# An adaLN transformer block on one core: V projected first, fewer filling matmuls, sums of four norms on VectorE, a new order

## The chip, the core and the metric

The kernel runs on one core of a Trainium2 chip. Its engines run side by side, each through its own queue of instructions in order: TensorE (PE in the profile, with PEld for its weight loads), VectorE (DVE), ScalarE (ACT), GpSimd (POOL) and SyncE (SP). ACT and SP also issue the transfers (DMA); these stand in the engine's queue like any other instruction. Matmul results land in PSUM, which DVE and ACT read. The metric is the device time of one execution in microseconds (us); lower is better.

## What is computed

A sequence of 2048 tokens of width 448 goes through a block of attention and feed-forward. A vector c gives six modulation vectors: shift and scale for each norm, and a gate for each half. Attention is local and dilated: each of 16 heads of width 28 looks at 8 tokens, two apart, its own included.

```python
    x = A_x
    mod = (_silu(c) @ w_mod).reshape(c.shape[0], 6, 1, -1)
...
    h = _layernorm(x, axis=-1) * (1 + ca) + sa
    x = x + ga * _A_ref(h, A_wqkv, A_wo)
    h = _layernorm(x, axis=-1) * (1 + cb) + sb
    x = x + gb * _B_ref(h, B_w1, B_w2)
```

`_A_ref` projects to Q, K and V with `wqkv`, takes a softmax over the positions 0, 2, ..., 14 behind each token, and projects with `wo`; `_B_ref` is silu(h `w1`) `w2` with a hidden width of 1792. sa, ca, ga, sb, cb, gb are the six parts of `mod`.

Tensors are bfloat16, sums are kept in float32.

## The kernel before

**Tiling.** Even and odd tokens are two streams of 1024, since the dilation is 2 and the streams never meet. The first part of the work goes in four chunks of 256 token pairs (`NC = 4`): load of x, first norm, Q/K projection. V and the attention go in nine units (`NU = 9`) of two windows of 57 queries and 64 keys. The second half goes in eight blocks `m` of 128 token pairs for the output projection and second norm, and in four groups `k` for the FFN.

**Names of the steps**, with the lines of the profile:

- Loads (L240): `ldx0a`, `ldx0b`, `ldx1` to `ldx3` (x), `ldc` (c), `ldm_a0/1` (the part of w_mod with the first shift and scale, 672 and 224 KB), `ldm_b0/1` (the rest, 1344 and 448 KB), `ldwqk0/1`, `ldwv0/1`, `ldwo0/1`, `ldw1..`, `ldw2..`. Each is one issue on SP or ACT.
- `tab` is ACT's table load, `silu_c` (L299) the silu of c, `ccol` (L303) four tiny matmuls that lay it out, `scT` its copy. `mod1.mm` and `mod2.mm` (L319, 32 matmuls each) give shift and scale in columns, `ga.mm` and `gb.mm` (L337) the gates.
- `warm` and `junk0` to `junk21` (L294) are the filling matmuls: on a zeroed tile, into a PSUM tile that nobody reads.
- First norm of block `m`, `n1m`: `st0/1` (L358, L359: bn_stats and bn_aggr on DVE), `rstd` (L371, L372 on POOL), `nm`, `xn0/1` (L390 on ACT or L392 on DVE: the normalized rows). The first two blocks are turned on TensorE (`h00.trp`, `h01.trp`, L451), and the modulation is applied on the way out of PSUM: `h00.mod0/1`, `h01.mod0/1` (L235 on ACT, L237 on DVE), two quarters of the width each. Later blocks are turned by DMA (`.tr`, L409) and modulated in place.
- `pad0..3` (L437) spread the Q/K weights to heads of 32 columns. `qkKg.S/.C` (L478) project chunk K, head group g, in two halves of 8 and 6 matmuls; `.ev` (L482) takes the result out of PSUM. `vU.S/.C` (L495) project V of unit U in 16 and 12 matmuls; `.ev` (L500).
- `lgU` (L533) logits of unit U, into two PSUM tiles; `exU0/1` (L540) exponentials on ACT, one for each tile; `mkU` (L591) mask; `avU` (L607) product with V; `rcU`, `onU` (L614, L619) division; `otrU` (L622) DMA transpose; `alU` (L628) copy into place.
- `woM.S/.C` (L658) output projection of block M, `resM` (L666) residual on DVE, which leaves the row sums beside it. Second norm `n2m`: either `s`: `mean` (L365) from those sums and two squares on ACT (`sq`, L368), or `b`: bn_stats on DVE as in the first norm. `HOW2` says which for each block.
- `gK.mod` modulation, `f1Ki` (L687) first FFN matmuls of group K, 7 pairs, with silu out of PSUM on ACT (L692); `f2M` (L712, and L724 in the last block) second FFN matmuls; `yaM` (L747) residual; `stoM` (L752, L754) store.
- At the end a check that no softmax sum left its range: `checkmm`, `flag`, and `read`, which every engine executes (L831), ahead of a branch to a slower version.

**Order.** Each step is an object in a list; its number is its place there. The string `ORDER` names all of them in the order in which they are emitted, each with a letter for its engine (p PE, a ACT, v DVE, g POOL, s SP). It fixes every engine's queue; waits between engines follow from the data. There are four PSUM tiles, handed out and taken back in that order, so a matmul step also waits for the engine that empties the tile it gets.

The order before begins so. TensorE: `warm`, three `junk`, `ccol`, ten `junk`, `mod1.mm`, `h00.trp`, `h01.trp`, nine `junk`, the eight halves of `qk0`, `v0`, `v1`, `lg0`, then `qk1` mixed with `lg1`. ACT: `ldx0a`, `ldx0b`, `ldm_a0`, `ldwqk1`, `tab`, `silu_c`, `scT`, `ldwv1`, `n10.xn0/1`, `pad2`, `h00.mod0`, `h01.mod0`. SP: `ldc`, `ldx1`, `ldm_a1`, `ldwqk0`, `ldx2`, `ldwv0`, `ldx3`. DVE takes `h00.mod1` and `h01.mod1`.

Of the kernel before, what the change touches and what calls it, by code (L numbers as in the profile page):

```python
# [39 lines left out]
23g 30p 21g 34p 27g 36p 40p 0a 64v 63v 1a 3a 2s 8a 20a 69v 70v 53a 54p 55a 6a 9s 33p 4s 41p 44p 7s 65g 29g 37p 49p 52p 35p 66v 67a 71g 72g 112v 111v  # L40
73v 74v 39p 42p 68a 38p 57p 75p 78p 58v 10s 5s 62v 47p 51p 32p 61a 50p 48p 24g 43p 46p 76a 77v 80v 45p 31p 11s 59v 60v 105v 106v 79a 113g 15a 85p 114g
115a 86g 168v 93p 116a 118s 87p 107g 94g 169v 108v 109v 110a 210v 163v 162v 117s 81p 89p 82g 95p 22g 90g 25g 26g 83p 88a 91p 12s 164g 13s 96a 97p 101p
98g 102g 92v 56v 84a 250p 251a 252a 165v 119v 122v 121v 99p 103p 100a 120v 127p 123p 166v 104v 28g 170g 171v 167a 172v 211v 173v 259p 124g 128g 129p
125p 260a 261a 131p 132g 135p 253v 126a 130a 205v 204v 174s 175s 136g 133p 262v 134a 137p 138a 143p 254p 206g 139p 140g 144g 177a 178v 212g 179v 255v
256v 263p 145p 141p 147p 146a 16s 14s 149p 264v 265v 176v 213v 214v 142a 148a 273p 150a 180p 184p 207v 181g 182p 185g 274a 275a 183a 287p 208v 209v
288a 289a 215v 186p 153v 154v 192p 188p 193g 217s 216s 266s 257s 194p 276v 220a 221v 187v 219v 189g 290v 190p 277p 196p 195a 267a 258a 278v 279v 218v
191a 200p 197g 198p 201g 202p 291p 199v 203a 268p 292v 293v 301p 269g 270p 302a 303a 19s 280s 281v 230p 272v 282p 271v 231g 343g 283g 315p 284p 304v
316a 232p 286v 285v 350v 226p 233v 305p 227g 317a 228p 345a 344a 306v 294s 295v 318v 352a 229a 351a 17s 18s 222p 223g 234p 235g 224p 307v 346g 236p
347g 225v 308s 237a 319p 348a 320v 353g 354v 321v 246p 247g 329p 248p 238p 239g 330a 249a 331a 242p 240p 156v 309v 349v 243g 322s 357s 355v 356v 241a
151p 244p 332v 333p 310p 152v 323a 155v 358s 324p 311g 334v 335v 336s 362v 312p 314v 313v 161v 444v 296p 325g 326p 297g 359a 361a 360a 245a 298p 299v  # L50
300v 159v 437v 327v 363p 364g 445a 383p 365p 384g 366a 385p 387p 388g 386a 367p 389p 368g 446a 337v 158v 328v 338p 375p 447g 376g 369p 377p 439a 390a
# [90 lines left out]
def layer(ctx, tc, io, safe):  # L142
# [13 lines left out]
    def ct(shape, name, dt=BF16):  # L156
        return const.tile(shape, dt, name=name)
# [15 lines left out]
    junk = ct([128, 512], "junk")  # L173
# [26 lines left out]
    ps = [psum.tile([128, 2, 512], F32, name=f"ps{i}") for i in range(4)]  # L200
# [20 lines left out]
    P = Plan()  # L221
# [66 lines left out]
    misc_ready = [pool_op("rcone", lambda: G.memset(rc[:], 1.0), "rcone"), pool_op("ones", ones, "ones")]  # L288

    def warm_up(o, n):  # L290
        t = ps[w_first["slot"]["ps"][0]]
        for _ in range(n):
            for j in range(2):
                matmul(t[:, j, :], lhsT=junk[half(j), 0:128], rhs=junk[half(j)], start=True, stop=True)  # L294
# [4 lines left out]
    sc_op = P.op("silu_c", "a", "silu_c", lambda o: S.activation(out=sc7[:], in_=c7[:], func=ACTF.Silu), [ld_c, tab])  # L299
# [475 lines left out]
    for k in range(1, NC):  # L775
# [6 lines left out]
        if k == 1:  # L782
# [3 lines left out]
            eng = {"dve": V, "pool": G}  # L786
# [101 lines left out]
```

## Time and profile before

| | us |
|---|---|
| median of 3 runs | 179.65 (178.55 to 180.41) |
| the profiled execution | 179.35 |
| its span, first to last instruction | 177.5 |
| outside the span | 1.85 |
| mean granted clock of TensorE | 0.979 |

The profile is of one execution. Its busy times are for an engine's instructions, and those of PE overlap a little, since matmuls are pipelined. A row of the timeline gives start, length, engine, line, operation, tiles and count; in brackets the idle time of the engine before it and who ended it. Lines that carry the argument are shown in the prediction.

### The profile page before, as it was taken

To read this page: it belongs to the slowest core of one execution; us is meant where nothing else is said; L and a number is where in the kernel's file an instruction comes from. 1 tells how busy PE (TensorE), PEld (TensorE's weight loads), DVE (VectorE), ACT (ScalarE), POOL (GpSimd) and SP (SyncE) were. 2 spreads that over 40 slices of the span, in tenths; PEclk is the share of its full clock that TensorE was granted. 3 is DMA by queue.
4 is the path that set the end of the run, shared out by engine and by line. 5 is a ranking of instruction groups with operands and counts; after the bars stand their busy time and mean duration, and the time that the engine had idled before them with its cause. 6 is when DMAs were issued, how large, how long until landed. Compare 5 with 4: busy or idle time off the path is not lost.

```text
span 177.5 us, 6130 instructions
## 1 busy us (share of the span) xinstructions
PE 161.1 (91%) x2716; PEld 84.3 (47%) x2716; DVE 84.6 (48%) x186; ACT 101.0 (57%) x136; POOL 23.6 (13%) x68
## 2 busy tenths in 40 slices
PE   7885998996899999989999999999999999999920
PEld 2252454453465555635555644455444444554710
DVE  3929579585678887696053870050623000020420
ACT  3345488974785868399896768967144662400000
POOL 7722260110000140001110400013000000000000
PEclk9998799999999999999999999999999999999995
DMA  5993792979965976630009038300140000010240
GB/s 185 392 357 84 145 375 65 140 242 92 153 185 109 289 150 80 134 59 4 0 21 105 4 59 199 34 2 4 42 128 4 0 0 4 0 52 4 103 153 21
DMA packets 32351, 18.54 MB, mean 104 GB/s; under 512 B 25022, under 2 KB 31294, under 8 KB 32318
## 3 DMA queue, kind: packets, MB, share of 16 engines
q1 hardware_dynamic: 30334, 15.67, 38.7%
q10 hardware_dynamic: 1984, 2.41, 4.3%
q8 instruction: 23, 0.38, 0.9%
q14 instruction: 10, 0.08, 0.2%
HBM read 10.21 MB, written 1.84 MB: 68 GB/s over the span
## 4 chain that ended last, share of the span: by engine, by line
PE 77%; DMA 8%; ACT 5%; DVE 3%; issue 3%; ACTq 1%; DVEq 0%
PE ps L687 24%; PE ps L712 21%; PE ps L478 15%; DMA wqk<-in_A_wqkv_dram 5%; PE ps L658 4%; PE ps L495 4%; PE ps L533 3%; PE ps L724 3%; PE ps L607 3%; DMA h<-xn 3%; ACT p L540 1%; ACT h L235 1%; ACT ho L235 1%; PE ps L337 1%; ACTq L240 1%
## 5 line engine op out<-in xcount | busy, mean ns | idle before, releaser
L712 PE MATMUL ps<-w,both 64*128 64x448 bf16 x392 | 39.2, 349 | 0.0
L692 ACT ACTIVATE both<-ps 128x1024 bf16<-128x1024 f32 x28 | 27.6, 1021 | 19.6 <-PE ps L687 19.5
L687 PEld LDWEIGHTS <-w 64*128 64x128 bf16 x392 | 19.8, 94 | 23.1 <-issue 1.8
L478 PE MATMUL ps<-ho,wp 64*128 64x512 bf16 x224 | 27.6, 395 | 3.2 <-ACT ho L235 2.5
L712 PEld LDWEIGHTS <-both 64*128 64x128 bf16 x392 | 19.0, 94 | 17.9
L747 DVE TENSOR_TENSOR ot<-ps,x_all 128x896 bf16<-128x896 f32 x6 | 6.5, 1090 | 38.1 <-issue 20.6
L687 PE MATMUL ps<-h,w 64*128 64x512 bf16 x196 | 23.0, 376 | 0.8 <-issue 0.5
L687 PE MATMUL ps<-wqk,w 64*128 64x512 bf16 x196 | 22.3, 376 | 0.0
L540 ACT ACTIVATE p<-ps 128x912 bf16<-128x912 f32 x18 | 15.9, 929 | 7.8 <-PE ps L533 7.8
L478 PEld LDWEIGHTS <-wp 64*128 64x128 bf16 x224 | 12.0, 98 | 16.5 <-issue 3.5
L482 ACT CAST qk<-ps 128x1024 bf16<-128x1024 f32 x12 | 11.8, 1014 | 5.4 <-PE ps L478 5.4
L495 PE MATMUL ps<-wv,ho 64*64 64x448 bf16 x252 | 13.7, 352 | 0.0
L666 DVE SCALAR_TENSOR_TENSOR x_all<-ps,x_all 128x448 bf16<-128x448 f32 x16 | 9.5, 619 | 8.5 <-PE ps L658 8.5
L591 DVE TENSOR_TENSOR p<-p,maskb 128x1824 bf16<-128x1824 bf16 x9 | 10.1, 1121 | 5.4 <-ACT p L540 5.3
L390 ACT ACTIVATE xn<-x_all,nm,rs 128x512 bf16<-128x512 bf16 x12 | 9.4, 811 | 4.9 <-POOL nm L380 2.7
L658 PE MATMUL ps<-wo,ho 64*128 64x448 bf16 x112 | 12.2, 350 | 0.0
L372 POOL TENSOR_TENSOR rs<-rs,negh 128x2 f32<-128x2 f32 x16 | 11.3, 708 | 1.3
L368 ACT ACTIVATE scr<-x_all,mv 128x448 bf16<-128x448 bf16 x16 | 10.6, 665 | 0.9 <-POOL mv L365 0.7
L371 POOL TENSOR_SCALAR rs<-mv 128x2 f32<-128x2 f32 x16 | 3.1, 197 | 56.6 <-ACT scr L368 21.0
L358 DVE BATCH_NORM_STATS2 st<-x_all 128x6 f32<-128x448 bf16 x16 | 9.7, 605 | 1.9 <-DMA x_all<-in_A_x_dram 1.9
L619 DVE TENSOR_TENSOR o<-ps,rc 121x896 bf16<-121x896 f32 x9 | 9.8, 1091 | 0.3
L294 PE MATMUL ps<-junk 64*128 64x512 bf16 x56 | 8.8, 472 | 1.2 <-DVE junk L202 1.2
(79 smaller groups left out, 144.7 us busy)
## 6 DMA issues: line engine op xcount, KB each, us to landing
w<-in_B_w_dram SPq DMA_DIRECT2D x2, 896.0 KB, 5.4
w<-in_B_w_dram SPq DMA_DIRECT2D x2, 784.0 KB, 7.5
x_all<-in_A_x_dram SPq DMA_DIRECT2D x3, 448.0 KB, 8.3
both<-in_w_mod_dram SPq DMA_DIRECT2D x1, 1344.0 KB, 6.6
out_dram<-ot SPq DMA_DIRECT2D x6, 224.0 KB, 1.9
both<-in_w_mod_dram ACTq DMA_DIRECT2D x1, 672.0 KB, 6.9
x_all<-in_A_x_dram ACTq DMA_DIRECT2D x2, 224.0 KB, 3.2
wqk<-in_A_wqkv_dram ACTq DMA_DIRECT2D x1, 448.0 KB, 8.9
```

What stands on the lines that cost most here:

```text
L368: S.activation(out=scr[:], in_=x_all[:, us[t], :], func=ACTF.Square, bias=mv[:, t, 0:1], accum_out=mv[:, t, 1:2])
L372: G.tensor_tensor(out=rs[:], in0=rs[:], in1=negh[:], op=ALU.pow)
L478: return [matmul(t[:, j, :], lhsT=w, rhs=hT[rows, :, kt, s0:s0 + CP], start=start, stop=stop)]
L482: copy_on(o)(out=qk[:, :, g, :, s0:s0 + CP], in_=t[:].rearrange("p j (t s) -> p j t s", t=2))
L495: return [matmul(t[half(par), j, 0:D], lhsT=hT[rows, par, kt, k0:k0 + KB], rhs=wv[rows, kt, :], start=start, stop=stop) for par in range(2)]
L540: S.activation(out=p_of[u][:, 2 * t * w:2 * t * w + 2 * w].rearrange("p (j n) -> p j n", j=2), in_=bank(a, t)[:, :, 0:w], func=ACTF.Exp, s ...
L591: V.tensor_tensor(out=p, in0=p, in1=m, op=ALU.mult)
L619: V.tensor_tensor(out=dims(t[0:n, :], 0, (576, 2), (DH, H), (1, DH)), in0=view(bank(a))[:, :, :, 0:DH], in1=r, op=ALU.mult)
L658: x = matmul(t[:, par, 0:D], lhsT=oT[rows, par, i // 2, 128 * m:128 * m + 128], rhs=wo[rows, j, :], start=(j == 0), stop=(j == 5))
L687: return [matmul(t[:, i // 7, :], lhsT=w1[rows, kt, 128 * i:128 * i + 128], rhs=h[rows, :, kt, :], start=start, stop=stop)]
L692: S.activation(out=hid[:, k % 2, :, i, :], in_=t[:], func=ACTF.Silu)
L712: x = matmul(t[:, par, 0:D], lhsT=hid[half(hf), k % 2, jj, ii, 128 * j:128 * j + 128], rhs=w2[half(hf), ii + 7 * jj, :], start=(way == 0 a ...
```

## The change

Four things change. `HOW2` puts the sums of the last four second norms (blocks 4 to 7) from ACT's squares to bn_stats on DVE. The `junk` steps may be put on SP, where they do nothing; 17 of the 22 are. `ORDER` is a new one. With `HOW2` the list has four steps fewer, so the numbers behind that place shift.

```diff
-HOW2 = "ssssssss"
+HOW2 = "ssssbbbb"
...
 ORDER = """
...
     def warm_up(o, n):
+        if o["eng"] == "sp":
+            return
         t = ps[w_first["slot"]["ps"][0]]
         for _ in range(n):
             for j in range(2):
                 matmul(t[:, j, :], lhsT=junk[half(j), 0:128], rhs=junk[half(j)], start=True, stop=True)
     w_first = P.op("warm", "p", "warm", lambda o: warm_up(o, WARM), take=("ps",), group=("P", "w", 0))
-    junks = [P.op(f"junk{i}", "p", "junk", lambda o: warm_up(o, 1), [w_first], group=("P", "w", 0)) for i in range(JUNK)]
+    junks = [P.op(f"junk{i}", "ps", "junk", lambda o: warm_up(o, 1), [w_first], group=("P", "w", 0)) for i in range(JUNK)]
```

The new order in names, where it differs most:

```text
PE, start    ccol warm junk16 junk19 junk10 junk6 mod1.mm h00.trp h01.trp junk0 v0.S v1.S v0.C v1.C
             qk00.S qk02.S qk01.S qk03.S qk02.C qk01.C qk03.C qk00.C ga.mm mod2.mm lg0 lg1
             qk11.S qk13.S qk10.S qk11.C qk12.S qk10.C qk13.C qk12.C av1 v2.S lg2 v2.C av0 v3.S gb.mm lg3
ACT, start   ldc tab ldm_a1 silu_c ldm_a0 ldwqk1 ldwqk0 ldm_b1 ldm_b0 n10.xn0 n10.xn1 n11.xn1
             h00.mod1 pad3 pad2 n12.xn0 v1.ev qk02.ev qk01.ev qk00.ev ex00 ex01 ex10 ex11
SP, start    ldx0a ldx0b ldx1 ldwv0 ldwv1 ldx2 n12.tr n13.tr ldx3 ldwo0 n15.tr n14.tr
DVE, start   n10.st0 n10.st1 n11.st1 n11.st0 n10.nm scT n12.st0 n11.nm n11.xn0 n12.st1 mod1.ev
             h00.mod0 h01.mod1 h01.mod0 pad0 pad1 n13.st0 n13.st1 n12.xn1 v0.ev n13.xn0 n13.xn1
POOL, start  rcone vone0 ozero0 masks n10.rstd n11.rstd ozero1 n12.rstd
PE, to FFN   wo1.C qk33.S qk31.S qk33.C qk31.C av3 v6.S av4 v6.C v8.S v7.S v8.C v7.C lg5
             qk30.S qk32.S wo2.S qk32.C qk30.C wo2.C f100.S lg6 f100.C f102.S f105.S wo3.S
PE before    wo1.C qk32.C qk31.S av4 qk31.C qk30.S qk33.S qk30.C qk33.C av5 v8.S lg6 v8.C v6.S v7.S v6.C
             mod2.mm v7.C av6 wo3.S wo4.S wo3.C wo2.S wo4.C wo2.C f100.S
end, SP      sto4 sto6 read sto5 sto71        (before: sto4 sto0 sto6 sto3 read sto72)
end, ACT     sto70 read sto72                 (before: sto71 read sto70)
```

More of the change, by code (lines that the diff above doesn't have):

```diff
@@ new lines @@
+42s 98g 101p 38s 99p 25g 102g 29g 23g 103p 43s 113g 81p 89p 90g 104a 100v 85p 93p 91p 94g 86g 114g 115v 82g 87p 116v 56v 92a 88a 95p 83p 147p 151p 10s
+168v 169v 117s 163v 162v 170g 171g 84a 172v 96v 250p 148v 152v 259p 118s 120v 121v 122v 119v 164g 11s 211v 165v 251a 252a 260a 261a 210v 166v 127p
+135p 123p 15a 128g 124g 136g 129p 131p 167a 130a 125p 137p 173v 205v 204v 262v 132g 253v 133p 14s 263p 175s 126a 134a 212g 139p 174s 140g 138v 273p
+264v 265v 213v 17a 141p 177v 254p 274a 206g 142a 255v 256v 214v 176v 275a 179v 143p 178a 149p 144g 150a 287p 145p 288a 146a 215a 289a 266s 257s 207v
@@ L61 @@
+583v 581v 543p 584v 535p 493s 536a 605p 597p 606g 598g 544a 589p 607p 608a 590g 593p 599p 594g 600a 585p 586g 595p 591p 592a 596a 609p 610g 587p 611p
+549p 558p 550p 551p 612a 588a 613p 552g 601p 559p 602g 603p 553p 560p 561g 554p 562p 614p 604a 563p 615p 564p 616g 617p 618p 619p 555p 622p 623p 624p
+625p 620v 556v 565v 557s 626v 621s 628v 627a 630v 633p 634v 635p 566s 631a 629s
 """
```

35 lines of the change are left out of this document (14 added, 21 removed).

## The prediction

> **What bounds the kernel now.** I read four views in this order: the page's shares and slices, the busy time by stretch, the chain of waits, and the timeline of the first 15 us.
>
> First the page: busy time of each engine, and the transfer rate in 40 slices of 4.44 us.
>
> ```profile
> PE 161.1 (91%) x2716; PEld 84.3 (47%) x2716; DVE 84.6 (48%) x186; ACT 101.0 (57%) x136; POOL 23.6 (13%) x68
> ...
> GB/s 185 392 357 84 145 375 65 140 242 92 153 185 109 289 150 80 134 59 4 0 21 105 4 59 199 34 2 4 42 128 4 0 0 4 0 52 4 103 153 21
> ```
>
> TensorE (PE) is busy 91% of the span, but that hides where it is not. The stretches show it; columns are length, then busy us (instructions) of PE, PEld, DVE, ACT, POOL, then granted clock, DMA share, GB/s.
>
> ```profile
> 0.00:15.06 15.06, 10.75 (x109) 4.93 (x110) 8.44 (x27) 5.70 (x10) 7.67 (x30) 1.00 0.78 275
> 15.06:23.25 8.19, 8.13 (x60) 3.76 (x63) 5.16 (x16) 4.94 (x7) 2.77 (x7) 0.79 0.69 164
> 23.25:78.03 54.78, 50.44 (x1428) 28.51 (x1425) 42.33 (x81) 39.46 (x52) 6.66 (x14) 1.00 0.76 162
> 78.03:164.14 86.11, 86.11 (x1080) 43.05 (x1080) 25.17 (x58) 50.87 (x70) 6.52 (x18) 1.00 0.18 34
> 164.14:169.66 5.52, 5.52 (x46) 4.06 (x44) 2.18 (x2) 0.00 (x0) 0.00 (x0) 1.00 0.26 99
> 169.66:177.50 7.84, 0.11 (x2) 0.00 (x1) 1.27 (x4) 0.00 (x0) 0.00 (x0) 0.74 0.28 87
> ```
>
> From 15.06 (first Q/K projection) to 169.66 (last matmul) PE is the bound: 154.60 us, of which it idles 0.06 + 4.34 + 0 + 0 = 4.40. Before lie 15.06 us of loads, first norm and filling matmuls; behind, a tail of 7.84. So only four things can move the end: the start of useful matmuls, the clock, the 4.40 of idle, the tail.
>
> The clock, in stretches cut where it changes:
>
> ```profile
> 12.97:16.39 3.42, 1.27 (x11) 0.65 (x13) 3.34 (x11) 1.95 (x4) 0.00 (x0) 1.00 0.12 24
> 16.39:19.80 3.41, 3.41 (x19) 1.50 (x17) 3.27 (x12) 1.90 (x3) 0.90 (x2) 0.50 0.73 180
> 40.27:43.69 3.42, 2.14 (x70) 1.27 (x71) 1.87 (x3) 1.60 (x3) 0.00 (x0) 1.00 1.20 119
> ```
>
> After a stretch in which PE was busy 1.27 of 3.42 us the granted clock is 0.50 for 3.41 us, which costs 3.41 x 0.5 = 1.7 us of the first Q/K projection. After one with 2.14 busy of 3.42 it stayed at 1.00.
>
> The chain of waits and the timeline say what sets 15.06:
>
> ```profile
> 11.93 1.02 ACT ho L235 x2
> ...
> 12.98 1.38 DVE ho L237 x4
> ```
> ```profile
> 1.24 4.02 PE L294 MATMUL ps<-junk 64*128 64x512 bf16 x18 [1.24 <-DVE junk L202]
> ...
> 1.69 0.46 ACTq L240 DMA_DIRECT2D both<-in_w_mod_dram  x1
> ...
> 3.62 0.38 SPq L240 DMA_DIRECT2D x_all<-in_A_x_dram  x1
> ...
> 4.01 0.26 ACT L299 ACTIVATE sc<-c 7x64 bf16<-7x64 bf16 x1
> ...
> 6.74 1.52 ACT L390 ACTIVATE xn<-x_all,nm,rs 128x512 bf16<-128x512 bf16 x2 [1.07 <-DVE nm L378]
> ...
> 8.68 0.95 PE L319 MATMUL ps<-scT,both 128*128 128x1 bf16 x32 [0.60 <-DMA both<-in_w_mod_dram]
> ...
> 9.49 1.05 PE L451 MATMUL ps<-ident,xn 128*128 128x128 bf16 x16
> ...
> 10.48 2.12 PE L294 MATMUL ps<-junk 64*128 64x512 bf16 x18
> ...
> 11.09 0.94 ACT L437 COPY wp<-wqk 128x896 bf16<-128x896 bf16 x1 [2.83 <-DMA wqk<-in_A_wqkv_dram]
> ...
> 14.44 0.56 ACT L235 ACTIVATE ho<-ps,modc 128x256 bf16<-128x256 bf16 x1 [1.50 <-DVE ho L237]
> ...
> 15.06 8.15 PE L478 MATMUL ps<-ho,wp 64*128 64x512 bf16 x56 [2.46 <-ACT ho L235]
> ```
>
> w_mod lands at about 8.6, the modulation columns (L319) and transposes (L451) follow by 10.54; ACT first pads the late Q/K weights (L437), and only then the modulated rows are written, ACT and DVE taking turns (L235, L237, with waits of 1.50), until 15.06.
>
> **The change, part by part.**
>
> *V first.* Its 56 matmuls (two window pairs) need wv and the four modulated parts, not the Q/K weights. These rows price it:
>
> ```profile
> 23.13 1.71 PE L495 MATMUL ps<-wv,ho 64*64 64x448 bf16 x32
> ...
> 25.40 1.33 PE L495 MATMUL ps<-wv,ho 64*64 64x448 bf16 x24
> ```
> ```profile
> x_all<-in_A_x_dram SPq DMA_DIRECT2D x3, 448.0 KB, 8.3
> ...
> both<-in_w_mod_dram ACTq DMA_DIRECT2D x1, 672.0 KB, 6.9
> ...
> wv<-in_A_wqkv_dram ACTq DMA_DIRECT2D x1, 224.0 KB, 7.0
> ```
> ```profile
> SPq L240 <- DMA x_all<-in_A_x_dram: 1.9, 2, 1.0
> ```
>
> Start: on ACT the 672 KB of w_mod now stand behind the silu of c, so they are issued after c has landed, near 3.6 instead of 1.69 (the 3.62 row also shows the ninth transfer waiting for an early one; this may be the ninth). By the slices 0.82 MB move by 4.44 and 0.39 MB a us after that. Ahead of w_mod's end lie x0 0.448, x1 0.448, wv 0.448 and w_mod 0.896, 2.24 MB: 4.44 + 1.42/0.39 = 8.1; with x2 too, 9.2. I take 8.5, next to today's 1.69 + 6.9 = 8.6. Then 0.95 (L319) to 9.45 and half of the 1.05 (L451) to 10.0. DVE writes two parts of the first 128 tokens in 0.69 (half of 1.38), then ACT two in 1.02, since the rows show the two engines taking turns on one PSUM tile; the second tile's parts fall to DVE alone, beside ACT. V starts at 10.0 + 0.69 + 1.02 + 0.2 for hand-overs = 11.9. Lower end 11.2 (no turn-taking, w_mod at 8.1); upper end 13.4 (all four strictly in turn). I take 11.9 because the second tile belongs to one engine.
>
> Queues that these steps move past: SP now carries x0, x1, wv and x2 ahead of the first transposes, and x3 behind them, where it is needed first at about 25. POOL sets rc before the first norm's root instead of at 25:
>
> ```profile
> 25.02 0.52 POOL L288 MEMSET rc<- 128x288 f32 x1 [1.39 <-PE ps L495]
> ```
>
> That puts ACT's two normalized rows at 7.2 instead of 6.74, to 8.7, still 0.7 ahead of the transposes at 9.45.
>
> V lasts 1.71 + 1.33 = 3.04, to 14.9, and Q/K follow without a gap: the Q/K weights (0.896 MB) land at 4.44 + (2.24 + 0.448 + 0.896 - 0.82)/0.39 = 11.5, their pads end by 11.75 + 2 x 0.94 = 13.6 on ACT. The cover is 1.3 us. So useful work starts 15.06 - 11.9 = 3.16 us earlier. V is moved, not added; where it stood (23 to 27, under the table load and exponentials) TensorE then has a gate and the second modulation columns, which it does today at 38 to 40 and 70 to 71: no more in sum. Their 1.79 MB of w_mod land at about 4.44 + (3.58 + 1.79 - 0.82)/0.39 = 16.1 and are needed at 21.4.
>
> *Filling matmuls.* 17 of 22 become nothing: 34 of 56 matmuls. The 20 that stand between c's columns and L319 take 20 x 4.02/18 = 4.5 us at the slow pace, from about 3.8 to 8.3, so they hide in the wait for w_mod. One pair stands before V; PE then waits about 10.8 to 11.9. In any 3.41 us PE idles at most some 1.3, nearer the 2.14-busy row than the 1.27-busy one, so I take clock 1.00 and the 1.7 us come back. Ends: 0 back, 1.7 back.
>
> The Trainium skill's "TensorE: Matmul & The Clock Gate" (section "What's actually happening") says that the clock falls only after an idle window of about 3.4 us. The trace disagrees: it fell after a wait of 2.46. By that page a wait of 1.1 is safe, as by my rows, and the sum stays. The same section asks for a busy window of about 3.4 us before the clock rises; by that rule 4.5 us of filling hold a whole window only if its phase is kind, and otherwise V starts slowly, the rival below with 176.6.
>
> *Sums on DVE for the last four second norms.* It removes 8 squares on ACT and adds 8 statistics on DVE:
>
> ```profile
> L368 ACT ACTIVATE scr<-x_all,mv 128x448 bf16<-128x448 bf16 x16 | 10.6, 665 | 0.9 <-POOL mv L365 0.7
> ...
> L358 DVE BATCH_NORM_STATS2 st<-x_all 128x6 f32<-128x448 bf16 x16 | 9.7, 605 | 1.9 <-DMA x_all<-in_A_x_dram 1.9
> ...
> L359 DVE BATCH_NORM_AGGREGATE mv<-st 128x2 f32<-128x6 f32 x16 | 2.9, 182 | 0.5
> ```
>
> 8 x 0.67 = 5.3 us leave ACT (50.87 busy of 86.11 there) and 8 x 0.79 = 6.3 come to DVE (25.17 of 86.11). PE idles 0.00 in that stretch: worth 0, covered by DVE's 61 us of slack. Without the cover the FFN's next block would wait, up to 6.3.
>
> *New order up to the first FFN.* From 15.06 to 78.03 it is one in-order puzzle of four PSUM tiles. Now both first logits run back to back and hold all four tiles, so the next four Q/K halves wait for exponentials; in return the first FFN matmul comes before one more logits, two attention products and two output projections, PE work that then fills later waits:
>
> ```profile
> L658 PE MATMUL ps<-wo,ho 64*128 64x448 bf16 x112 | 12.2, 350 | 0.0
> ...
> L533 PE MATMUL ps<-qk 28*64 28x57 bf16 x576 | 6.9, 200 | 2.9 <-issue 2.9
> ...
> L607 PE MATMUL ps<-v,p 64*57 64x29 bf16 x576 | 6.0, 179 | 0.0
> ```
>
> Two of 8 projections, one of 9 logits, two of 9 products: 3.05 + 0.77 + 1.33 = 5.2 us. I cannot show the new idle from a row. Low end 1, if every wait is filled; high end 9, if the stretch doubles its 4.34. I take 4.4, what the same work idles today.
>
> *Tail.* Today the last stores are:
>
> ```profile
> 170.70 1.35 ACTq L754 DMA_DIRECT2D out_dram<-wqk  x2
> ...
> 171.96 0.34 SPq L754 DMA_DIRECT2D out_dram<-wqk  x1
> ```
>
> SP issues its last one at 171.96, behind the read of the flag. In the new order a 224 KB store stands between that read and SP's last: one more issue, 0.4 us (0 to 0.8).
>
> *Sum.* V at 11.9, plus PE work 154.60 - 4.40 - 1.70 = 148.5, plus idle 4.4, gives 164.8; plus tail 7.84 + 0.4 = 173.0. The profiled execution took 179.35 for a span of 177.5, 1.85 outside: 174.9. That execution is 0.3 under the median 179.65.
>
> **The rivals.**
>
> *The clock falls or never rises ahead of V.* For: far fewer filling matmuls. Against: the 40.27 row. V's start falls into a slow window: + 1.7, 176.6; two windows, 178.3.
>
> *The new order idles more.* PE's gain only meets ACT or DVE: for it, DVE is busy 42.33 and ACT 39.46 of 54.78 in that stretch, and four tiles are all there is. Idle 8.4 instead of 4.4: 178.9, no change. Both would have to fit into the 47 us from 21.4 to 68. Against: with 5.2 us of PE work and what hangs on it moved behind, each stays near four fifths.
>
> *The new order idles less.* Idle 1 to 2: 171.5 to 172.5. For: nothing after 78.03 waits today, and of the 4.34 ahead of it 1.28 lie in one place, the 40.27 row.
>
> *Slower: the first norm is held on ACT's queue.* Its first two normalized rows (6.74, 1.52) now stand behind seven transfer issues on ACT. If a transfer from the ninth on waits for the one eight before it (3.62 row), the last issue could wait for Q/K weights at 11.5: rows to 13.7, transposes to 14.2, modulation to 16.2, V at 16.4, and PE waits of 4 and 2 us, thus the slow clock: 174.9 + 4.5 + 1.7 = 181.1. It decides against the change once V starts after about 14.9 with a slow window, or 16.4 without. Against: counting in order, that last issue waits for an early x or V transfer, landed by about 8.
>
> *By the page "DMA: Bandwidth & Descriptors" (section "Queues, rings and completion order") of the Trainium skill* each engine serves the two queues in turn, so fetching V's weights and x first would slow w_mod; the 8.1 to 9.2 above holds that already.
>
> **How the numbers follow.** A measurement of this kernel tells about 1% from no change (177.9 to 181.4). Chances: forecast 0.50 (own range 173 to 177), clock 0.12, more idle 0.18, less idle 0.10, ACT's queue 0.10. Faster by over 1%: 0.50 + 0.10 + 0.08 of the clock case = 0.68. Within: 0.04 of clock and 0.15 of more idle = 0.19. Slower: 0.03 + 0.10 = 0.13. The range 171.0 to 179.5 takes in less idle, clock and most of more idle, and leaves out ACT's queue and the extremes.
>
> **What would show each step.** V's matmuls (L495) first at 11.2 to 13.4, Q/K (L478) right behind within 0.3; L319 at 8.1 to 9.2; granted clock 1.00 from V on; the first FFN matmul (L687) near 11.9 + (8.13 + 50.44 - 1.7 - 5.2) + 4.4 = 68 instead of 78.03; PE without a wait from there on; no ACT squares among the last four norms; 8.2 from last matmul to end. I am wrong if Q/K wait for their weights, if the clock reads 0.50 after 11.9, or if idle after V's start exceeds 8.

## The result and the profile after

The changed kernel took 185.38 us (median of 4 runs, 184.57 to 188.53), the kernel before 179.53 on the same chip: ratio 1.0315, 95% interval 1.0259 to 1.0371. Here and below a median takes all runs of a kernel, and a ratio only the runs within 1.5% of the kernel's fastest, so the two can differ by up to 1%. The forecast was 174.9, and its range ended at 179.5. So the change is 3% slower, and the forecast missed by 10.5 us. The profiled execution took 184.65 for a span of 182.9.

The page of the changed kernel, the same lines as before: shares, granted clock in 40 slices (4.57 us each), transfer rate.

```profile
PE 160.1 (87%) x2682; PEld 83.3 (46%) x2682; DVE 90.9 (50%) x208; ACT 97.0 (53%) x120; POOL 21.4 (12%) x62
...
PEclk9965999996999789999999999999999999999995
...
GB/s 183 309 401 314 117 189 109 99 232 61 127 103 388 150 0 103 134 4 0 4 84 79 77 64 56 4 77 138 52 162 4 4 0 0 4 0 4 100 68 50
```

PE's share fell from 91 to 87% although its work did not grow. The clock line has dips in three places instead of one. The stretches (length, then busy us of PE, PEld, DVE, ACT, POOL, granted clock, DMA share, GB/s) tell where:

```profile
0.00:14.37 14.37, 7.81 (x75) 4.09 (x75) 7.36 (x24) 4.22 (x6) 8.47 (x29) 0.88 0.88 302
14.37:25.01 10.64, 10.64 (x115) 4.87 (x114) 9.22 (x24) 5.74 (x8) 3.38 (x11) 0.84 0.70 214
25.01:40.00 14.99, 12.15 (x421) 7.82 (x420) 11.38 (x26) 11.55 (x14) 1.88 (x4) 1.00 0.66 146
40.00:50.15 10.15, 7.96 (x236) 4.45 (x237) 5.37 (x10) 5.80 (x9) 0.00 (x0) 0.83 0.62 92
50.15:61.67 11.52, 8.80 (x82) 4.04 (x82) 5.78 (x10) 6.17 (x7) 0.00 (x0) 1.00 0.96 257
61.67:78.55 16.88, 16.37 (x414) 8.97 (x415) 12.96 (x29) 12.01 (x19) 1.77 (x4) 0.90 0.40 65
78.55:174.76 96.21, 96.21 (x1347) 49.10 (x1342) 37.59 (x86) 51.48 (x62) 5.92 (x14) 1.00 0.21 44
174.76:182.90 8.14, 0.11 (x2) 0.00 (x1) 1.27 (x4) 0.00 (x0) 0.00 (x0) 0.71 0.23 66
```

From 78.55 on, PE waits for nothing, as forecast. Ahead of it lie idle times of 2.84, 2.19, 2.72 and 0.51, 8.26 in sum, and three stretches with a clock below 1.00. The waits of PE up to there (sum, times, longest) name the places:

```profile
PE ps L321 <- DMA both<-in_w_mod_dram: 3.5, 1, 3.5
PE ps L305 <- ACT sc L301: 3.1, 1, 3.1
PE ps L609 <- issue: 3.0, 1, 3.0
PE ps L660 <- DVE ho L630: 2.7, 3, 1.7
PE ps L480 <- DVE st L360: 1.8, 1, 1.8
PE ps L535 <- DVE qk L484: 0.5, 1, 0.5
```

(Lines behind the junk function are two higher than before: L319 is L321, L495 is L497, L607 is L609. In the kernels of the experiments they shift by one: L320, L496, L608.) The timeline, ACT's rows and then PE's:

```profile
2.80 0.25 ACT L301 ACTIVATE sc<-c 7x64 bf16<-7x64 bf16 x1
2.81 0.40 ACTq L240 DMA_DIRECT2D both<-in_w_mod_dram  x1
```
```profile
3.31 4.39 PE L296 MATMUL ps<-junk 64*128 64x512 bf16 x20
11.15 1.02 PE L321 MATMUL ps<-scT,both 128*128 128x1 bf16 x32 [3.45 <-DMA both<-in_w_mod_dram]
12.03 1.87 PE L453 MATMUL ps<-ident,xn 128*128 128x128 bf16 x16
13.83 0.61 PE L296 MATMUL ps<-junk 64*128 64x512 bf16 x2
14.37 4.49 PE L497 MATMUL ps<-wv,ho 64*64 64x448 bf16 x56
18.79 6.22 PE L480 MATMUL ps<-ho,wp 64*128 64x512 bf16 x56
```
```profile
38.39 0.53 PE L609 MATMUL ps<-v,p 64*57 64x29 bf16 x44
41.88 0.44 PE L609 MATMUL ps<-v,p 64*57 64x29 bf16 x20 [2.96 <-issue]
...
56.26 0.93 PE L660 MATMUL ps<-wo,ho 64*128 64x448 bf16 x8 [0.50 <-DVE ho L630]
...
60.10 0.93 PE L660 MATMUL ps<-wo,ho 64*128 64x448 bf16 x8 [1.69 <-DVE ho L630]
...
61.67 0.70 PE L535 MATMUL ps<-qk 28*64 28x57 bf16 x60 [0.50 <-DVE qk L484]
...
78.39 1.03 PE L689 MATMUL ps<-h,w 64*128 64x512 bf16 x8
```

The modulation weights land at 2.81 + 8.3 = 11.1, so V starts only 0.69 earlier than Q/K did before, and at half clock: 16 transposes take 1.87 instead of 1.05, V's 56 matmuls 4.49 instead of 3.04. Q/K follow without a gap. Then PE waits 1.76 ahead of the second chunk's Q/K (L480), 2.96 in the middle of 64 small products, where the profile shows nothing that it waits for ("issue"), and three times for the copies `al` on DVE (L630). Two of these copies start late, behind Q/K matmuls and a modulation:

```profile
55.80 0.40 DVE L630 COPY ho<-op 128x912 bf16<-128x912 bf16 x1 [2.68 <-PE ps L480]
...
59.64 0.40 DVE L630 COPY ho<-op 128x912 bf16<-128x912 bf16 x1 [2.92 <-ACT ho L235]
```

The first FFN matmul comes at 78.39; before it came at 77.35. (The prediction counts from the row behind that, 78.03, and the expectations below call 78.39 "78.55", by the cut of the stretches.)

Two of the half-clock stretches, cut where the clock changes:

```profile
14.34:17.76 3.42, 3.42 (x42) 1.71 (x44) 3.27 (x11) 2.97 (x5) 0.22 (x2) 0.50 0.88 345
41.65:45.07 3.42, 3.19 (x40) 1.24 (x40) 2.67 (x7) 0.00 (x0) 0.00 (x0) 0.50 0.21 45
```

Against the forecast sum, from the end of PE's work: 174.76 instead of 164.8. Of these 9.96 us, V's start makes 14.37 - 11.9 = 2.47, idle 8.26 - 4.4 = 3.86, and slower work 160.39 - 8.26 - 148.5 = 3.63. The last goes with three stretches of half clock from V's start on, of 3.4 us each, where the forecast had none.

### The profile page after: what moved, and what is told of

Read it like the earlier page. It is cut to its first block, busy times and chain, and to the rows that moved or that the text cites. A ratio compares the mean times of both kernels' runs of the same rounds, so it can differ in the third digit from the quotient of the medians.

```text
span 182.9 us, 6061 instructions
## 1 busy us (share of the span) xinstructions
PE 160.1 (87%) x2682; PEld 83.3 (46%) x2682; DVE 90.9 (50%) x208; ACT 97.0 (53%) x120; POOL 21.4 (12%) x62
## 3 DMA queue, kind: packets, MB, share of 16 engines
HBM read 10.21 MB, written 1.84 MB: 66 GB/s over the span
## 4 chain that ended last, share of the span: by engine, by line
PE 81%; DMA 6%; DVE 4%; ACT 3%; issue 2%; DVEq 0%; ACTq 0%
PE ps L689 23%; PE ps L714 20%; PE ps L480 14%; PE ps L497 6%; PE ps L660 6%; DMA both<-in_w_mod_dram 5%; PE ps L726 3%; PE ps L609 3%; PE ps L535 2%; PE ps L339 1%; DMA c<-in_c_dram 1%; PE ps L321 1%; PE ps L453 1%; DVE ho L237 1%; ACT p L542 1%
## 5 line engine op out<-in xcount | busy, mean ns | idle before, releaser
L689 PEld LDWEIGHTS <-w 64*128 64x128 bf16 x392 | 19.0, 94 | 22.3
L480 PE MATMUL ps<-ho,wp 64*128 64x512 bf16 x224 | 26.4, 387 | 2.1 <-DVE st L360 1.8
L689 PE MATMUL ps<-h,w 64*128 64x512 bf16 x196 | 22.3, 376 | 0.0
L749 DVE TENSOR_TENSOR ot<-ps,x_all 128x896 bf16<-128x896 f32 x4 | 4.3, 1085 | 32.3 <-issue 30.6
L480 PEld LDWEIGHTS <-wp 64*128 64x128 bf16 x224 | 11.9, 97 | 15.3 <-issue 3.8
L484 ACT CAST qk<-ps 128x1024 bf16<-128x1024 f32 x11 | 11.0, 1013 | 9.7 <-PE ps L480 9.7
L497 PE MATMUL ps<-wv,ho 64*64 64x448 bf16 x252 | 15.8, 397 | 0.0
L360 DVE BATCH_NORM_STATS2 st<-x_all 128x6 f32<-128x448 bf16 x24 | 14.6, 609 | 2.3 <-DMA x_all<-in_A_x_dram 2.3
L660 PE MATMUL ps<-wo,ho 64*128 64x448 bf16 x112 | 12.8, 361 | 2.7 <-DVE ho L630 2.7
L373 POOL TENSOR_SCALAR rs<-mv 128x2 f32<-128x2 f32 x16 | 3.1, 193 | 97.6 <-PE ps L689 38.4
L392 ACT ACTIVATE xn<-x_all,nm,rs 128x512 bf16<-128x512 bf16 x14 | 10.8, 809 | 6.5 <-DVE nm L380 6.5
L497 PEld LDWEIGHTS <-ho 64*64 64x64 bf16 x252 | 8.0, 120 | 4.7 <-issue 2.1
L660 PEld LDWEIGHTS <-ho 64*128 64x128 bf16 x112 | 5.2, 95 | 9.0 <-DVE ho L630 4.1
```

The costliest lines, as they stand in the source:

```text
L360: V.bn_stats(out=st[:], in_=x_all[:, us[t], :])
L392: S.activation(out=out_, in_=in_, func=ACTF.Identity, scale=rs[:, t:t + 1], bias=nm[:, t:t + 1])
L480: return [matmul(t[:, j, :], lhsT=w, rhs=hT[rows, :, kt, s0:s0 + CP], start=start, stop=stop)]
L484: copy_on(o)(out=qk[:, :, g, :, s0:s0 + CP], in_=t[:].rearrange("p j (t s) -> p j t s", t=2))
L497: return [matmul(t[half(par), j, 0:D], lhsT=hT[rows, par, kt, k0:k0 + KB], rhs=wv[rows, kt, :], start=start, stop=stop) for par in range(2)]
L660: x = matmul(t[:, par, 0:D], lhsT=oT[rows, par, i // 2, 128 * m:128 * m + 128], rhs=wo[rows, j, :], start=(j == 0), stop=(j == 5))
```

## The experiments

All times are medians; a ratio is against the kernel before, run on the same chip. The experiments ran on four chips, on which the kernel before took 179.2 to 179.9, so kernels of different groups are compared better by their ratios. Edits are shown as moves in the order of names.

**Four single edits of the changed kernel.** One for each suspected loss.

```diff
 e1_wmod_ahead, ACT
-tab ldm_a1 silu_c ldm_a0 ldwqk1
+tab ldm_a1 ldm_a0 silu_c ldwqk1
 e2_fill, PE
-junk6 mod1.mm
+junk6 junk15 junk3 junk4 junk21 junk9 junk20 junk14 junk18 mod1.mm
 e3_copies_early, DVE: al1 right behind al0, al2 ahead of wo0.S in the whole order
-al0 ... al1 ... al2
+al0 al1 ... al2
 e4_load_later, ACT: 896 KB
-ldw11 ... h3.mod0
+h3.mod0 ldw11
```

> The changed kernel with one move: the fetch of the modulation's weights, ldm_a0, is issued on ACT's queue ahead of the silu of c instead of behind it. Theory (the fetch lands at 11.1 because its issue waited 0.9 us for c): issue at 1.9 instead of 2.81, landing at 9.7 to 10.3, V's matmuls start at 13.0 to 13.6 instead of 14.37, the time falls by about 1 us against the changed kernel's 185.4. Rival (the x and V weights that are issued ahead of it on SP's queue set the landing): landing within 0.4 us of 11.1, no change of the time.

> The changed kernel with 16 of the filling matmuls (8 pairs) put back on PE ahead of the modulation's matmuls, so that the wait from 7.7 to 11.15 us is filled; each works on constants and leaves the output as it is. Theory (the missing filling work lets the clock fall ahead of V): the granted clock reads 1.00 from the first transposes on, L453's 16 transposes take 1.05 us instead of 1.87, V's 56 matmuls 3.1 instead of 4.49, Q/K ends at 22.5 to 23.0 instead of 25.01, the time falls by about 2 us. Rival (later waits in the new order swallow it): the same early gain, but the first FFN matmul stays within 0.5 us of 78.55 and the time within 0.5 us.

> The changed kernel with the two copies that bring the odd heads' output to the right partitions, al1 and al2 (L630 on DVE), moved up in the order: al1 right behind al0, al2 right ahead of the output projection wo0. Theory (where the order puts them they wait for matmuls that they do not need, and PE waits for them at 55.8, 58.4 and 61.2): those three waits, 2.7 us in sum, go, with them the slow window at 62 to 65.5, the first FFN matmul comes 2 to 4 us earlier than 78.55 and the time falls by about 3 us. Rival (the copies then wait for the transposes of the attention output, or other work of DVE takes their place): the waits move and the time falls by less than 1 us.

> The changed kernel with one 896 KB weight load of the FFN, ldw11, issued about 17 us later on ACT's queue (behind the modulation of the third chunk instead of at 35.9). Theory (PE's wait of 2.96 us at 38.92, which no semaphore ends, comes from that load running beside the products): the wait shrinks under 1 us, the slow window of 41.6 to 45.0 goes with it, the first FFN matmul comes 2 to 4 us earlier and the time falls by 3 to 4 us. Rival (the wait comes with the dense run of small matmuls itself): a wait of 2 to 3 us stays between 38 and 42 and the time stays within 0.7 us.

| kernel | us | ratio (95%) | L321 starts | V starts | first FFN matmul | PE idle between |
|---|---|---|---|---|---|---|
| changed | 185.38 | 1.0315 (1.026 to 1.037) | 11.15 | 14.37 | 78.39 | 8.26 |
| modulation weights ahead of the silu | 183.29 | 1.0243 (1.013 to 1.036) | 9.62 | 13.19 | 75.44 | 7.93 |
| 16 filling matmuls back | 180.93 | 1.0109 (1.001 to 1.021) | 10.50 | 12.62 | 75.21 | 7.60 |
| copies early | 180.41 | 1.0102 (1.002 to 1.019) | 10.16 | 13.37 | 72.48 | 5.48 |
| FFN load later | 180.57 | 1.0057 (1.000 to 1.012) | 10.76 | 13.97 | 74.31 | 6.15 |

Starts and idle are of one profiled execution each. L321, which starts when the modulation weights have landed, varies between 10.16 and 11.15 in kernels that don't touch their fetch, so up to 1 us of an earlier start may be chance. The fetch edit did what its theory said at the start (9.62). With the copies early the waits of PE on L660 at 56 to 60 are gone, and so is the slow window behind them. With the load late the wait in the small products shrinks from 2.96 to 1.04 and doesn't vanish; the next paragraph asks why.

**What the wait without a semaphore is.** PE stops in that place in all of these kernels. In the changed kernel, above, it is behind 44 of 64 products, and so it is in every kernel of the new order with 22 filling matmuls. With the 16 filling matmuls, the timeline of PE shows:

```profile
37.74 0.36 PE L608 MATMUL ps<-v,p 64*57 64x29 bf16 x28
40.22 0.44 PE L608 MATMUL ps<-v,p 64*57 64x29 bf16 x36 [2.11 <-issue]
```

It comes after 28, exactly 16 matmuls earlier, as in every kernel here that has these 16: the place is fixed by the number of PE instructions since the start and not by data. The wait of 1.76 us ahead of the second chunk's Q/K looks like the same thing. The profile puts it down to a DVE statistic (L360) that those matmuls don't read; but it lies 256 matmuls ahead of the other one, and with the 16 filling matmuls it moves into the logits before it, where it reads 2.09 us of "issue". The transfer view has a queue of its own for instructions, 23 packets and 0.38 MB in all, 16 KB each. In the stretch around the wait, 38.4 to 41.9 in the changed kernel, and 36.5 to 39.5 with the load late (queue, packets, MB, share of 16 engines):

```profile
q1 hardware_dynamic: 699, 0.18, 67.1%
q10 hardware_dynamic: 187, 0.61, 44.8%
q8 instruction: 1, 0.02, 1.7%
```
```profile
q1 hardware_dynamic: 531, 0.14, 23.3%
q8 instruction: 1, 0.02, 2.4%
```

In the first, one such packet comes while 0.61 MB of the FFN weights move; in the second, only small transposed pieces stand beside it. The packet moves at 39.7 in the first, when PE already stands still, and at 36.8 in the second, before it does; PE goes on 2.1 and 2.6 us later. A packet at 26.9 lies as far, 2.7 us, ahead of the end of the wait of 1.76. That the packet is the fetch of PE's next instructions is an inference, but place and time agree: a long row of small matmuls uses up a fetched block faster than the next one comes. The effect of the load is shown: with it in its old place the wait is 1.84 to 2.96 us (five kernels of this order), with it late 0.75 to 1.04 (five). So the theory of the load holds for 1.9 of the 2.96 us, and 1.0 stays without it, as its rival said.

**All four, and the fetch put first.**

```diff
 e5_all: the four edits above
 e6_all_fetch: the four edits, with the first of them in this form
-SP   ldx0a ldx0b ldx1
+SP   ldc ldx0a ldx0b ldx1
-ACT  ldc tab ldm_a1 silu_c ldm_a0 ldwqk1
+ACT  ldm_a0 tab ldm_a1 silu_c ldwqk1
```

> The changed kernel with the four edits of the first four runs together: the modulation's weights issued ahead of the silu, 16 filling matmuls back, the two copies early, the FFN load late. Theory (the change lost by three separate places: a start no earlier than before, PE's waits with the slow clock behind them, and it would have had the forecast 174.9 us without these): V's matmuls start at 12 to 12.6, no half clock between the first transposes and the last FFN matmul, PE idle after V's start 3 to 4 us, first FFN matmul at 69 to 71, time 174 to 176. Rival (the four edits cure one and the same slow window, so that their gains do not add): 178.5 or more, with the first FFN matmul past 72.

> As the run of the four edits together, and the fetches at the start reordered: c first on SP's queue, the 672 KB of modulation weights as the first transfer on ACT's queue, before everything else there. Theory (the landing of that transfer sets V's start): issued at 0.8, it lands at 8.0 to 9.2, V's matmuls start 0.8 to 1.5 earlier than in that run, and the time is about 1 us lower. Rival (x then comes later, and the first norm or the transposes set V's start; or the rate is shared out so that the landing stays): V's start within 0.4 of that run's and the same time.

The four together took 178.99, ratio 0.9858 (0.980 to 0.992), first FFN matmul at 72.33 in a profiled execution of 179.37; with the fetch first 177.18, ratio 0.983 (0.977 to 0.990), and 71.04. The second, called the best version below, is faster than the kernel before. Whether the first is, stays open, since its median lies only 0.5% below the kernel before on that chip (179.86). The two are not told apart by these intervals. The gains of the single edits do not add: by the medians 2.1 + 4.4 + 5.0 + 4.8 would be 16, and it was 6.4; by the ratios 13, and it was 8. The rival had that right. With the fetch first, the 672 KB land 4.3 us after an issue at 0.79 instead of 8.3 after 2.81, so well ahead of PE's use; and yet V starts at 12.30, against 12.09 with the four edits alone:

```profile
8.88 0.94 PE L320 MATMUL ps<-scT,both 128*128 128x1 bf16 x32 [0.23 <-DVE scT L306]
...
10.36 0.40 PE L452 MATMUL ps<-ident,xn 128*128 128x128 bf16 x4 [0.30 <-ACT xn L391]
10.92 0.62 PE L452 MATMUL ps<-ident,xn 128*128 128x128 bf16 x8 [0.16 <-DVE xn L393]
...
12.30 0.70 PE L496 MATMUL ps<-wv,ho 64*64 64x448 bf16 x8 [0.44 <-DVE ho L236]
```

PE now waits in turn for the normalized rows and the modulated rows: x and the first norm took the place of the weights, the rival's case.

**Start and later part apart.** Since the gains did not add, two kernels split them.

```diff
 e13_start_only: the changed kernel
+fetches of e6_all_fetch
+16 filling matmuls of e2_fill
 e14_later_only: the changed kernel
+copies of e3_copies_early
+load of e4_load_later
```

> The changed kernel with the edits of the start alone: c first on SP's queue, the modulation's weights as the first transfer on ACT's, 16 filling matmuls back. Theory (start and later part cost separately, about 3 us each): V's matmuls start at 12 to 12.8, the first FFN matmul 2.5 to 4 us earlier than 78.55, time 181 to 182.5. Rival (a gain at the start is swallowed by later waits): time 184 or more.

> The changed kernel with the edits of the later part alone: the two copies early and the FFN load late. Theory (they cost separately from the start): V's matmuls still start at 13.3 to 14.4, the waits at 38.9, 55.8, 58.4 and 61.2 are gone or under 1.1, no half clock between 33 and the last FFN matmul, first FFN matmul at 73 to 75.5, time 179 to 181. Rival (the two cure one and the same slow window, so that the pair is worth no more than one of them): time 181 or more.

The start alone: 181.80, ratio 1.0178 (1.009 to 1.026), V at 12.28, first FFN matmul at 74.73. The later part alone: 177.43, ratio 0.9877 (0.983 to 0.992), first FFN matmul at 71.43 in a profiled execution of 178.54, V at 13.76. So two moves in the later part of the order turn 3% slower into 1% faster, and better than expected; the edits of the start, worth 3.6 us by themselves (2.5 by the ratios), add nothing that can be measured on top of them (177.18 against 177.43).

**V first, undone.** The central part of the change, in the best version and in the changed kernel.

```diff
 e9_qk_first (from e6_all_fetch), e10_after_qk_first (from the changed kernel), PE; v0.ev and v1.ev move along
-v0.S v1.S v0.C v1.C qk00.S qk02.S ... qk03.C qk00.C ga.mm
+qk00.S qk02.S ... qk03.C qk00.C v0.S v1.S v0.C v1.C ga.mm
```

> The kernel with the four edits and the reordered fetches (the run before this batch that took 177.2 us), with one part of the change undone: V of the first tokens (56 matmuls and their evictions) stands behind the Q/K projection again. Theory (V first fills the time in which Q/K waits for its padded weights, which were ready at 15.35 there): PE's first projection starts at 14.5 to 15.4 instead of 12.3, PE waits 2 to 3 us ahead of it, and the time is 2 to 4 us higher. Rival (later waits swallow the earlier start, so that the order of the two is worth nothing): within 0.8 us of 177.2.

> The changed kernel with that one part undone alone: V of the first tokens behind the Q/K projection. Theory (V first is worth the time until the padded Q/K weights are ready, 16.5 in the changed kernel): the first projection starts at 15.3 to 16.5 instead of 14.37 and the time is 1 to 2.5 us higher than the changed kernel's 185.4. Rival (with modulation weights that land at 11, V first gains nothing, since the late landing holds both): within 0.8 us of 185.4.

184.48 against 177.18, and 190.96 against 185.38: V first is worth 7.3 and 5.6 us in this order (8.8 and 7.0 by the ratios), more than either theory gave it. In the first of the two:

```profile
14.14 1.03 PE L479 MATMUL ps<-ho,wp 64*128 64x512 bf16 x4 [2.33 <-DVE wp L438]
15.35 8.13 PE L479 MATMUL ps<-ho,wp 64*128 64x512 bf16 x52 [0.18 <-ACT wp L438]
23.41 2.84 PE L496 MATMUL ps<-wv,ho 64*64 64x448 bf16 x56
27.27 0.92 PE L338 MATMUL ps<-both,screp 128*128 128x448 bf16 x4 [1.01 <-ACT v L501]
...
31.31 1.41 PE L534 MATMUL ps<-qk 28*64 28x57 bf16 x124 [2.20 <-DVE qk L483]
```

PE waits 2.5 us for the padded weights, the clock falls (8.13 us for 52 matmuls; V first had 6.22 for 56), and evictions hold up the next PSUM tile and the logits: 1.01 for V's on ACT, 2.20 for one of Q/K that stands behind V's on DVE. So within this order V first pays. The rest of the order stayed as it was built for V first; what V first is worth by itself the two runs don't say, and the kernel before, with Q/K first in an order of its own, took 179.5.

**The filling matmuls.** Left out alone from the kernel before, and from the best version.

```diff
 e7_before_less_fill: the kernel before
-junk0 to junk21 on PE
+junk2, 3, 5, 9 and 16 on PE, the other 17 on SP, where they are no instruction
 e12_fetch_no_fill: e6_all_fetch
-16 filling matmuls of e2_fill
```

> The kernel before with one part of the change alone: 17 of its 22 filling pairs left out, so that 22 filling matmuls stay, as many as in the changed kernel, in the same two places. Theory (the filling matmuls hold the clock ahead of Q/K): the granted clock falls to half for 3.4 to 7 us between 9 and 19, the first matmuls of Q/K take 1.5 to 2 times their 1.28 us for 8, and the time rises by 1.7 to 3.5 us over the kernel before. Rival (the clock falls in the wait ahead of Q/K in the kernel before too, so that the filling does nothing): no more than 0.5 us.

> The kernel with the four edits and the reordered fetches (177.2 us), without the 16 filling matmuls that it has back, so with the 22 of the changed kernel. Theory (filling matmuls matter where PE's work follows them without a long wait, as it does here): half clock for at least 3.4 us between 8 and 19, the 16 transposes or V's 56 matmuls take 1.3 to 2 times their 1.05 and 3.05 us, time 1 to 3 us higher. Rival (the wait is short now, 7.5 to 8.9, and the clock holds): no half clock there, the time within 0.8 us.

180.06 against 179.86, ratio 1.0052 (1.000 to 1.011), and 177.13 against 177.18 (ratios 0.989 and 0.983, with intervals that overlap). Neither costs anything that these intervals show. In the best version without filling, the start is slow and PE's next work is not:

```profile
10.36 1.59 PE L452 MATMUL ps<-ident,xn 128*128 128x128 bf16 x12 [0.20 <-ACT xn L391]
...
12.42 3.59 PE L496 MATMUL ps<-wv,ho 64*64 64x448 bf16 x56
15.94 6.22 PE L479 MATMUL ps<-ho,wp 64*128 64x512 bf16 x56
```

The transposes and V are slower, as the theory said, but V's last matmul still ends at 16.0, and Q/K begin at 15.94, as with filling (15.95): there V waited twice for modulated rows (0.44 and 0.28), so filling bought a clock that it could not use. In the changed kernel the filling did gain; there the transposes and most of V lay in 6.8 us of half clock.

**Second norms' sums on VectorE, alone.**

```diff
 e8_before_dve_norms: the kernel before, blocks 4 to 7
-HOW2 = "ssssssss"
+HOW2 = "ssssbbbb"
-n24.mean n24.sq0 n24.sq1 (ACT) ...
+n24.st0 n24.st1 (DVE, in the places of the squares) ...
```

> The kernel before with one part of the change alone: the sums of the last four second norms on VectorE (two batch-norm passes each) in place of the mean and the two squares on ScalarE. Theory (it is off the path that sets the end): the time within 0.7 us of the kernel before, PE without a wait from the first FFN matmul on. Rival (VectorE's longer queue holds the last norms back and PE waits for the transposed tiles): a wait of PE of 0.5 to 3 us in the last third, and as much more time.

181.40 against 179.86, ratio 1.0075 (1.004 to 1.011): slower by 1.3 us. The one wait of PE in the FFN, where the kernel before has none:

```profile
PE ps L686 <- DVE ot L746: 0.9, 1, 0.9
```

It ends at 137.6: DVE is late with a residual, and with it comes a PSUM tile late. The rival had the wait and its size, but not its place, since it expected PE to wait for a norm's transposed tiles. The other 0.4 us of the 1.3 the trace does not place. In the new order there is no such wait: the stretch 78.55 to 174.76 is full.

**The dense row of logits.** In the best version PE stopped 2.22 us inside the 128 small logit matmuls, up to 27.11, and the clock was at half from 26.7 to 30.1.

```diff
 e11_logits_apart (from e6_all_fetch), PE; ex10 and ex11 on ACT move along
-lg0 lg1 qk11.S qk13.S
+lg0 qk11.S lg1 qk13.S
 e15_mod_early (from e11_logits_apart), PE; mod2.ev on DVE moves along
-qk01.C qk03.C qk00.C ga.mm mod2.mm lg0
+qk01.C mod2.mm qk03.C qk00.C ga.mm lg0
```

> The kernel with the four edits and the reordered fetches (177.2 us), with the second half of the first logits (64 matmuls) and its two exponentials behind the first 8 Q/K matmuls of the second chunk. Theory (PE's wait of 2.22 us at 24.9, inside the run of 128 small logit matmuls, is the fetch of PE's own next 256 instructions, which a dense run uses up before they arrive; the slow window behind it comes from the wait): the wait shrinks under 1 us, no half clock at 26.7 to 30.1, time 1 to 2.5 us lower. Rival (the wait moves with the dense run or PE meets the first chunk's exponentials later): a wait of 2 us stays between 24 and 29, the time stays within 0.8 us or rises.

> The kernel with the four edits, the reordered fetches and the first logits in two parts (176.6 us), with the 32 one-column matmuls of the second modulation (L320) and their evictions moved ahead of the last 12 matmuls of the first Q/K projection. Theory (PE waits 1.06 us there for the second chunk's modulated rows, which wait for these matmuls; that wait in a run of small matmuls lets the clock fall): the wait shrinks under 0.4 us, no half clock at 25.4 to 28.8, time 1.5 to 2.5 us lower. Rival (the small matmuls alone let the clock fall, or PE now waits for the evictions of the first chunk that these matmuls covered): a half clock stays between 24 and 30, the time within 0.8 us.

With the logits apart, the wait shrank to 1.06 us (now for the modulated rows of the second chunk), the clock fell all the same at 25.4, and the time was 176.57, ratio 0.9877 (0.982 to 0.994), not told apart from 177.18. With the modulation early as well, the clock read 1.00 up to the last matmul, and the transposes and V ran at full speed too, in the only kernel here that did; yet it took 177.09, ratio 0.9894 (0.982 to 0.997). PE's wait for the modulated rows stayed (1.13 us), and 0.46 and 0.24 for evictions came in front. So at that place the clock was not what set the time: what PE gained, it waited for DVE and ACT (first FFN matmul at 69.96 with the half clock, at 70.06 without).

## Why the prediction was wrong, step by step

*V's start, 11.9 (11.2 to 13.4), was 14.37.* The step that failed is the landing of the modulation weights: 8.5 with bounds of 8.1 to 9.2, measured 11.1. I had the issue too late (3.6 against 2.81) and the transfer far too fast. I counted only the bytes ahead of it, 2.24 MB. By the slices, 0.183 x 4.57 + 0.309 x 4.57 = 2.25 MB had moved by 9.14, 1 us later than at my rate of 0.39, and 0.401 x 1.97 = 0.79 more by 11.11: 3.04 MB. The 0.8 MB more can only belong to transfers issued behind it, x2 at 3.20 and the weights from 3.51 on. So my bounds of 8.1 to 9.2 did not "hold already" what the two queues take from each other. Putting it first showed the same from the other side: 4.3 us from issue to landing instead of 8.3. What follows the landing came out at 3.2 us against 3.4, by luck. At full clock, with the filling back, it took 2.1 (10.50 to 12.62): V's first matmuls begin before ACT has written its two parts, which I had put ahead of them. The half clock made up for that, with 1.87 us of transposes.

*Q/K without a gap, the weights' pads hidden:* right in the changed kernel. That V first pays is borne out within the new order by the two runs that undo it; against the kernel before, its gain of 3.16 us came to 0.69.

*Filling matmuls, clock 1.00 from V on, 1.7 us back:* wrong. The clock was at half from 10.93 to 17.76, and again at 41.65 and 62.13 for 3.4 us each. The first stretch hangs on the landing: the filling ended at 7.7 and could not cover the 3.45 us that PE then stood until the late weights came. My rule from two rows of before (1.27 busy of 3.42 falls, 2.14 holds) was read for the start only. I never asked it of the waits that the new order would make later. The rival of the clock had the first window, and named V's start as its place; it did not see the other two, and priced two windows at 178.3.

*Idle after V's start, 4.4 (1 to 9), was 8.26.* The bounds held it, and the rival "the new order idles more" named 8.4, a close hit. But I priced that rival at 178.9, idle alone. In the trace most of the idle comes in three pieces of 1.7 to 3.0 us, and the clock fell with two of them; with the window at V's start, work was 3.63 us slower as well. And its mechanism was another: I argued with the total load of DVE and ACT, three quarters busy. The runs show two places in the order. The copies `al1` and `al2` waited for Q/K matmuls and a modulation that they need not wait for: put ahead of them, they did not. One 896 KB load ran beside a dense row of small matmuls. Moving both gave 7.9 us. My own forecast of the idle, "what the same work idles today", failed at the same point: I did not ask what that idle was. Of the 4.34 us before, 3.4 were already put down to "issue", and the prediction shows a row of logits with 2.9 of it.

*Sums on VectorE at nothing:* right for the new order, which keeps no wait behind 78.55; in the old order the same edit costs 1.3 us, so its price depends on the order around it.

*PE without a wait from the first FFN matmul, and 8.2 behind the last:* right (8.14). *First FFN matmul at 68:* 78.39, the sum of the misses above.

*The rival on ACT's queue* (first norm's rows behind seven issues) came true in part: those rows began at 8.09, right behind the last issue, but the late weights hid it.

The Trainium skill, "TensorE: Matmul & The Clock Gate" (section "What's actually happening"), asks for an idle window of about 3.4 us before the clock falls. The trace again disagrees: at 41.65 it fell 2.7 us into a wait of 2.96, and at 62.13 after pieces of 1.69 and 0.50.

What stays open is why the edits of the start gain 2.5 to 3.6 us alone and nothing on top of the later ones. Part of it may be chance: without an edit at the start, Q/K ended at 25.01 in the changed kernel and at 23.4 with the later edits, where the weights landed 0.4 earlier and one half-clock stretch of 3.4 us stood there instead of two. Of the 1.3 us that the start edits then still bring to Q/K's end (22.1), 0.4 arrive at the first FFN matmul (71.04 against 71.43), and an effect of that size these intervals can't show.

## What to carry to other kernels

Do not price a new order by the load of its engines, nor by the idle of the old order before you know what that idle is: list, for each instruction that PE will wait for, the one ahead of it in its queue, and each transfer that runs beside a row of small matmuls. A wait on TensorE costs itself and perhaps half of the next 3.4 us, so a rival that adds idle must be priced with the clock. A transfer lands by what runs beside it, not only by what was issued ahead; where one landing gates the start, issue it first, and then look for what is late next.

## What the runs showed of the hardware

**Where the clock falls is not told by PE's busy time alone.** Stretches of 3.4 us, the first and second with half clock right behind them, the third without:

```profile
38.24:41.65 3.41, 0.68 (x52) 0.50 (x44) 0.24 (x1) 2.92 (x4) 0.28 (x1) 1.00 1.14 241
```
```profile
21.98:25.39 3.41, 2.35 (x104) 1.94 (x104) 2.91 (x9) 3.37 (x5) 0.14 (x1) 1.00 0.55 138
```
```profile
39.64:43.05 3.41, 1.58 (x39) 0.82 (x40) 1.15 (x2) 1.76 (x3) 0.00 (x0) 1.00 0.96 127
```

They are of the changed kernel, of the one with the logits apart, and of the one with the copies early. The second was busy 2.35 us, but with 104 matmuls, most of them small logits or of one column; the third only 1.58, with 39. So the prediction's rule of busy time does not hold in general. The rise says the same: in the changed kernel PE was busy 3.19 us of the stretch 10.93 to 14.34, in 32 one-column matmuls, 16 transposes and 2 filling matmuls, and the next 3.42 us were still at half clock. That small matmuls count for less is a guess that fits, and was not tested.

**A clock that reads 1.00 may be no reading.** In the kernel before with less filling, the granted clock reads 1.00 up to 74.8, and still its first 16 transposes took 1.87 us, as at half clock in the changed kernel (1.05 at full). With the copies early it reads 1.00 up to 29.4, and they took 1.87 too. The profile seems to have no record of the clock it starts with, so here early stretches are judged by durations.

```profile
9.84 1.87 PE L452 MATMUL ps<-ident,xn 128*128 128x128 bf16 x16
```

**A wait that follows the count of instructions.** Waits put down to "issue" in rows of small matmuls moved with the count of PE's matmuls, by 16 for 16, and took 1.84 to 2.96 us beside a bulk load and 0.75 to 1.04 without it. That they are waits for PE's next instructions, fetched in packets of 16 KB, is inferred from the packet that moved 2.1 to 2.7 us ahead of the end of three of these waits.
